# Turned activations of the second token chunk through memory in 512-byte pieces: attention mixer with a gated MLP on one core

## The chip, the cores and the metric

The kernel runs on one core of a Trainium2 chip. The metric is the device time of one execution in microseconds (us), the median of several runs of the same program. A profile is one further execution, taken by the hardware profiler. The engines are TensorE (PE; its weight loads are PEld), VectorE (DVE), ScalarE (ACT), GpSimd (POOL) and SyncE (SP), which here issues every DMA, one after the other, in the order of its instruction list.

## The reference

All tensors are float32; `x` is one sequence of 2048 tokens with 512 channels.

```python
xn = _layernorm(x)
s  = A(xn, wqkv, wo)          # 32 heads of 16, causal window of 256, softmax, projection wo
g  = silu(B(xn, w1, b1, w2, b2))
return x + s * g

def B(x, w1, b1, w2, b2):     # 512 -> 1792 -> 512, per token
    y = _layernorm(x)
    h = gelu(y @ w1 + b1)     # tanh form
    return h @ w2 + b2
```

## The kernel before

*Arithmetic.* Every matmul of float32 data is done as three passes of a split value: a tile is held as a high part in a short format and a low part, the difference (`split`, lines 69 to 72: a copy by the named engine, then a subtraction on DVE). `PASSES` gives high-high, high-low, low-high.

*Stages.* The first stage (lines 811 to 849) is the attention over all heads, with the first chunk's MLP weights prepared beside it. The second stage, from line 852, works in four chunks of 512 tokens each, c = 0 to 3; only the chunks 0 and 1 are computed by the loop of lines 1081 to 1179, the chunks 2 and 3 together by the code from line 1181 on. The change concerns what chunk 0's pass prepares for chunk 1, and chunk 1's gelu.

*One chunk of the loop.* For a step i over the 14 groups of 128 hidden units, `activate` (line 1091) applies gelu on ACT to a hidden tile h of 128 units by 512 tokens, then splits it into `gh` (ACT's cast) and `gl` (DVE's subtraction); `project` (line 928) multiplies the group of the step before with `w2` into four PSUM banks `acc`, 12 matmuls; `hidden` (line 1086) makes a later group's h with 12 matmuls. In chunk 0 most hidden groups were made in the first stage, so that its last steps are `project` alone. After the loop `end_chunk` (line 938) adds the bias to `acc`, applies silu (`gated`), and multiplies by the attention's projection `s`, 48 matmuls, whose inputs `ohl` were prepared by DVE in the steps i = 8 to 13.

*The turned y.* The matmuls of `hidden` need the normalised tokens of their chunk with channels on the partitions. For chunk 1 the tokens are loaded into four tiles `y` (128 tokens by 512 channels each, line 872) and normalised once more: statistics on DVE and the application on ACT in the steps i = 3 and 4 of chunk 0. `turn_y(1, range(4))` (line 1129) then transposes each tile in place by DVE, in blocks of 32 by 32, and writes it to `z_d` in memory, one DMA of 128 rows of 2 KB for each tile. A transposition in blocks leaves the blocks themselves where they were; `fetch_y` (line 894) puts them in their places with four DMAs for each of the four channel groups kt, each of 512 pieces of 128 bytes: sixteen DMAs (lines 1136 and 1137). They land in `mlp["yy"][1][kt]`. Line 1139 splits these tiles in the steps i = 12 (kt = 0), 13 (kt = 1) and 14 (kt = 2 and 3); the profile names the tiles `yh` and `xnT`, after the buffers they lie in.

*The sums and the outputs of the attention.* In the same steps chunk 0 needs the attention outputs divided by their sums. The reciprocals of the sums (`den`) are made by DVE in four parts, in the steps i = 4 and 5, written to memory (`rden_d`, line 1134), and for each group g of eight heads, `load_o` (line 901) loads the outputs (`or`, 256 KB) and the reciprocals of eight heads, each repeated for 16 rows (`w<-rden_d`, 256 KB, into free parts of a `w2` buffer). DVE multiplies the two (line 1146) and splits the product (`split_o`).

*Order on the queues.* In the loop all engines, SyncE among them, run their instructions in the order in which the program issues them. Around the change SyncE's list is: four `z_d<-y`, `rden_d<-den`, then `or`, `w` four times in turn, the sixteen `xnT<-z_d`, and, from behind the loop, the four y loads for chunk 2 and the four `xo` loads of chunk 0's end. DMAs report to eight semaphores in turn, and each one waits until the DMA eight places ahead of it has landed. A tile of pool `t2` (5 buffers) or `yp` (4 buffers: `y`, and `or` in chunk 0) waits until the tile that held its buffer has been used up. The buffer with the tag `wa` holds, one after another, a weight (`wva`), y of chunk 0, split hidden tiles (`g_first`, used up in the steps i = 1 and 2 of chunk 0) and from the end of chunk 0 on `gated`.

All instructions are recorded by one helper, so the profile gives line 43 for each; tiles tell them apart.

Of the kernel before, what the change touches and what calls it, by code (L numbers as in the profile page):

```python
# [9 lines left out]
F32 = mybir.dt.float32  # L10
F32R = mybir.dt.float32r
I32 = mybir.dt.int32
AF = mybir.ActivationFunctionType
# [4 lines left out]
S, D, H, DH, WIN, F = 2048, 512, 32, 16, 256, 1792  # L18
P = 128
NCH = S // 512  # L20
# [30 lines left out]
def mixer_kernel(ctx, tc, x, wqk, wv, wo, w1, b1, w2, b2, out):  # L51


    nc = SimpleNamespace(**{name: Ordered(tc, name) for name in ("tensor", "vector", "scalar", "gpsimd", "sync")})

    const = ctx.enter_context(tc.tile_pool(name="const", bufs=1))
    bigp = ctx.enter_context(tc.tile_pool(name="bigp", bufs=1))
    t2 = ctx.enter_context(tc.tile_pool(name="t2", bufs=5))
    small = ctx.enter_context(tc.tile_pool(name="small", bufs=3))
    dram = ctx.enter_context(tc.tile_pool(name="dram", bufs=1, space=bass.MemoryType.DRAM))  # L60
# [8 lines left out]
    def split(dst_hi, dst_lo, src, eng=None):  # L69

        (eng or nc.scalar.copy)(dst_hi, src)
        nc.vector.tensor_sub(dst_lo, src, dst_hi.bitcast(F32))
# [4 lines left out]
    def load(pool, tag, src, name, shape=(P, 512)):  # L77
        t = pool.tile(list(shape), F32, tag=tag, name=name)
        nc.sync.dma_start(t, src)
        return t  # L80
# [102 lines left out]
    oT_d = dram.tile([4, 8, 32, S], F32, name="oT_d")  # L183
# [2 lines left out]
    w_d = {"w1": dram.tile([P, NF * 512], F32, name="w1_d"), "w2": dram.tile([P, NF * 512], F32, name="w2_d"),  # L186
           "wo": dram.tile([P, 4 * 512], F32, name="wo_d")}
    g_d = dram.tile([NF, P, 512], F32, name="g_d")
    z_d = dram.tile([NCH - 1, 4, P, 512], F32, name="z_d")
    mT_d = dram.tile([NQ, NCH, 32, P], F32, name="mT_d")  # L190


# [45 lines left out]
    b1s = const.tile([P, NF], F32, name="b1s")  # L238
# [346 lines left out]
    mlp = {}  # L585
# [54 lines left out]
    def y_steps(a, b):  # L640
        run(mlp["ln"][a:b])

    def hidden_mm(ps, f, k):
        kt, (a, b) = k // 3, PASSES[k % 3]
        nc.tensor.matmul(ps, w1_part(a, f)[:, P * kt: P * (kt + 1)], mlp["yy"][b][kt],
                         start=(k == 0), stop=(k == 3 * KT - 1))
# [49 lines left out]
    n, raw = raws["qk"]  # L696
# [176 lines left out]
    for f in range(6, NF, 2):  # L873
        t = gp.tile([P, 2, 512], F32, tag="ohl", name=f"hr_{f}", bufs=4)
# [12 lines left out]
    def turn_y(c, tiles):  # L887

        for i in tiles:
            y = mlp["y"][i]  # L890
            nc.vector.transpose(y, y)
            nc.sync.dma_start(z_d[c - 1, i], y)

    def fetch_y(c, kt, dst):

        for k in range(4):
            at = z_d[c - 1, 0, 0, 128 * kt + 32 * k: 128 * kt + 32 * k + 32]
            nc.sync.dma_start(dst[32 * k: 32 * k + 32].rearrange("p (t j) -> p t j", j=32),
                              bass.AP(tensor=at.tensor, offset=at.offset, ap=[[512, 32], [32 * 512, 16], [1, 32]]))

    def load_o(c, g):

        cols = slice(512 * c, 512 * (c + 1))
        pool, tag = (t2, "t2") if c else (mlp["yp"], "y")
        raw = load(pool, tag, oT_d[g, :, 0:DH, cols], f"or_{c}_{g}")
        rec = mlp["w2", g // 2][:, 512 * (14 + g % 2): 512 * (15 + g % 2)].bitcast(F32)
        nc.sync.dma_start(rec, bass.AP(tensor=rden_d.tensor, offset=rden_d.offset + 8 * g * S + 512 * c,
                                       ap=[[S, 8], [0, DH], [1, 512]]))
        return raw, rec

    def split_o(c, g, raw):
        ohl = gp.tile([P, 2, 512], F32R, tag="ohl", name=f"ohl_{c}_{g}", bufs=4)
# [6 lines left out]
    def open_accs(c):  # L919
        return [ps_mx.tile([P, 2, 512], F32, tag="mx", name=f"acc_{c}_{i}") for i in range(2)]  # L920

    def split_g(c, f, g, cast):
        gh = gp.tile([P, 512], F32R, tag="gh", name=f"gh_{c}_{f}")
        gl = gp.tile([P, 512], F32R, tag="gl", name=f"gl_{c}_{f}")
        split(gh, gl, g, cast)
        return gh, gl
# [154 lines left out]
    for c in range(2):  # L1081
        accs = open_accs(c)
        gs, os_, hs, wanted = {}, [], {}, []
        made = ready if c == 0 else {}

        def hidden(f):
            hs[f] = (ps_yt if c and f % 2 else ps_st).tile([P, 512], F32, tag="b", name=f"h_{c}_{f}")
            for k in range(3 * KT):
                hidden_mm(hs[f], f, k)

        def activate(f):
            if f in made and f in soon:
                gs[f] = made[f]
                return
            src = made[f] if f in made else hs.pop(f)
            g = src if f in made and f < 2 else t2.tile([P, 512], F32, tag="t2", name=f"g_{c}_{f}")
            nc.scalar.activation(g, src, AF.Gelu_apprx_tanh, bias=b1s[:, f: f + 1])
            gs[f] = split_g(c, f, g, nc.scalar.copy)

        order = [2, 3, 0, 1, 4, 5, *range(6, NF)] if c == 0 else [*range(NF)]  # L1100
        ahead = 2 + c
        for f in range(ahead if c else 0):
            hidden(f)
        o_from, o_late = (0, 0) if c else (7, 1)
        nc.sync.on = True
        for i in range(NF + 1):
            if i < NF:
                activate(order[i])
            if c and i in (1, 2, 6, 7):
                y_steps(6, 10)  # L1110
            if c and i >= 10 and i < 14:
                second_y(i - 10)
            if c and i == 14:
                kept["w"] = bigp.tile([P, 768], F32R, tag="wb1", name="wsh")
                combine_w(0)
            if c == 0:
                for kind, f in late_w[LATE[i]: LATE[i + 1]]:
                    settle(kind, f, nc.scalar.copy, nc.vector)
            if i >= 1:
                project(accs, [(order[i - 1], gs.pop(order[i - 1]))], order[0], order[-1])  # L1120
            if i + ahead < NF and order[i + ahead] not in made and order[i + ahead] > 1:
                hidden(order[i + ahead])
            if c == 0:
                if i == 3:
                    mlp["ln"] = layernorm(mlp["y"], "C1", True)
                    y_steps(0, 5)
                if i == 4:
                    y_steps(5, 10)
                    turn_y(1, range(4))
                if i in (4, 5):  # L1130
                    for j in (2 * i - 8, 2 * i - 7):
                        nc.vector.reciprocal(den[:, P * j: P * (j + 1)], den[:, P * j: P * (j + 1)])
                if i == 5:
                    nc.sync.dma_start(rden_d.rearrange("g a (c t) -> (g a c) t", c=NCH), den)
                    wanted += [load_o(0, g) for g in range(4)]
                    for kt in range(KT):
                        fetch_y(1, kt, mlp["yy"][1][kt].bitcast(F32))
                for kt in {12: (0,), 13: (1,), 14: (2, 3)}.get(i, ()):
                    split(mlp["yy"][0][kt], mlp["yy"][1][kt], mlp["yy"][1][kt].bitcast(F32))
            else:  # L1140
                steps2(i)
            k = i - o_from
            if 0 <= k - 2 - o_late < 4:
                os_.append(split_o(c, k - 2 - o_late, wanted[k - 2 - o_late][0]))
            if 0 <= k - 1 - o_late < 4:
                nc.vector.tensor_mul(wanted[k - 1 - o_late][0], *wanted[k - 1 - o_late])
            if c and 0 <= k < 4:
                wanted.append(load_o(c, k))
            if c == 0 and i == NF:
                mlp["y"] = load_y(2)  # L1150
            if c:
                if i in (2, 3, 7, 8):
                    turn_y(2 + i // 5, (0, 1) if i in (2, 7) else (2, 3))
                if i == 3:
                    mlp["y"] = load_y(3)
                    kept[0] = gated[:, 2:4]
                    kept[1] = bigp.tile([P, 2, 512], F32, tag="wb1", name="y2_21")
                    for kt in range(KT):
                        fetch_y(2, kt, kept[kt // 2][:, kt % 2])
                if i in (8, 9):  # L1160
                    for kt in (2 * i - 16, 2 * i - 15):
                        put("21" if kt > 1 else "11", kt % 2, kept[kt // 2][:, kt % 2])
                if i == 8:
                    fetch_second()
                if i == 12:
                    fetch_pair(0)
            if c and i in (0, 1, 5, 6):
                y_steps(5, 6)
        nc.sync.on = False
        if c == 0:  # L1170
            gated = bigp.tile([P, 4, 512], F32, tag="wa", name="gated")

        def between(i):
            if c == 1 and i in (1, 2):
                split_w(0, 2 * i - 2)
                split_w(0, 2 * i - 1)
        end_chunk(c, accs, os_, between)
        if c == 0:
            steps2(-1)
# [99 lines left out]
    for i in range(NF):  # L1279
# [9 lines left out]
        if 5 <= i < 9:  # L1289
            raw, rec = wanted  # L1290
# [37 lines left out]
```

## Time and profile before

| | us |
|---|---|
| median of 3 runs | 746.75 (746.61 to 747.2) |
| the profiled execution, its own time | 746.98 |
| span of the profile | 745.2 |
| ACT busy | 440.1 |
| DVE busy | 516.5 |
| POOL busy | 297.5 |

The granted clock of TensorE is 1.00 over the whole span. The page of the profile gives the busy time of each engine, the span in 40 slices, and the chain of work that ended last, followed back from the last instruction to whatever released it. Views of the trace give the same for a stretch: the chain in order of time, an engine's instructions with the idle time before each one and its releaser, groups of instructions by shape with the mean of one in ns, and busy times with the share that the 16 DMA engines were busy and the GB/s that they moved. Times in the views are us from the start of the span. A row "SPq" is SyncE's work of issuing a DMA, not the transfer.

### The profile page before, as it was taken

Reading aid. Unit: us, or ns where it says so; the run is one execution under the profiler, and the core shown is the slowest. Engines: PE = TensorE matmul, PEld = TensorE weight load, DVE = VectorE, ACT = ScalarE, POOL = GpSimd, SP = SyncE. Lnnn points to the kernel's source line nnn. Section 1 sums busy time; section 2 is a strip of 40 time slices with the busy share of each in tenths; the row PEclk is TensorE's granted clock in tenths of the full one; section 3 lists DMA queues with packets and bytes.
Section 4 is the critical chain, followed back from the end, with each engine's and each line's share of the span. In section 5 each row is a group of like instructions: output and inputs, shape, how many; then the busy total and the mean of one; then the engine's idle time right before and its main releaser. Section 6 shows DMA issues by size and latency. Waiting matters only on the chain.

```text
span 745.2 us, 18812 instructions
## 1 busy us (share of the span) xinstructions
PE 728.8 (98%) x7360; PEld 585.6 (79%) x7360; DVE 516.5 (69%) x790; ACT 440.1 (59%) x744; POOL 297.5 (40%) x644
## 2 busy tenths in 40 slices
PE   8999999999999999999999999999999999999997
PEld 7886777777778887777776688788888888888886
DVE  6886777877766678887773567656658755676643
ACT  7757767867667676778877756443544734442001
POOL 7413757757666555767867700020102000001102
PEclk9999999999999999999999999999999999999999
DMA  8633355757555624646735385745453322253611
GB/s 289 192 71 77 86 137 149 210 151 194 142 133 153 154 71 149 163 129 165 201 103 161 92 286 201 198 143 194 110 108 113 96 88 74 69 181 117 214 55 56
DMA packets 84025, 105.71 MB, mean 142 GB/s; under 512 B 36640, under 2 KB 36896, under 8 KB 83936
## 3 DMA queue, kind: packets, MB, share of 16 engines
q1 hardware_dynamic: 83936, 104.50, 49.5%
q8 instruction: 58, 0.95, 0.5%
q14 instruction: 31, 0.25, 0.1%
HBM read 54.53 MB, written 32.77 MB: 117 GB/s over the span
## 4 chain that ended last, share of the span: by engine, by line
PE 86%; ACT 5%; DVE 3%; DMA 2%; issue 1%; POOL 1%; SPq 1%; DVEq 0%; ACTq 0%; POOLq 0%
PE fb L43 19%; PE acc L43 17%; PE zo L43 12%; PE stb L43 9%; PE p L43 9%; PE s L43 6%; PE h L43 6%; PE xy L43 5%; ACT pt L43 4%; PE pv L43 3%; POOL pt L43 1%; DVE xy L43 1%; SPq L43 1%; DMA w<-rden_d 1%; DMA xnT<-z_d 1%
## 5 line engine op out<-in xcount | busy, mean ns | idle before, releaser
L43 POOL TENSOR_SCALAR_AFFINE_SELECT pt<-pt 128x256 f32<-128x256 f32 x480 | 192.9, 425 | 133.7 <-ACT pt L43 131.7
L43 ACT ACTIVATE pt<-stb 128x768 f32<-128x768 f32 (+1 forms) x244 | 188.5, 773 | 62.4 <-PE stb L43 55.1
L43 DVE TENSOR_REDUCE mt<-xy 128x4 f32<-128x1024 f32 (+1 forms) x128 | 152.6, 1192 | 4.4
L43 DVE COPY_PREDICATED xy<-upper,zo 128x512 f32<-128x512 int32 x112 | 77.8, 695 | 70.6 <-PE xy L43 63.1
L43 POOL TENSOR_TENSOR xo<-xo,gated 128x512 f32<-128x512 f32 x15 | 19.9, 1330 | 236.9 <-DVE gated L43 195.5
L43 PE MATMUL fb<-xnT,wqb 64*128 64x512 f32 (+1 forms) x684 | 104.6, 397 | 0.2
L43 PE MATMUL zo<-pt,vt 128*17 128x128 f32 x2880 | 103.7, 275 | 0.3 <-POOL pt L43 0.3
L43 PE MATMUL stb<-qk 64*128 64x384 f32 (+1 forms) x488 | 97.1, 393 | 6.2 <-ACT pt L43 3.9
L43 PE MATMUL acc<-w,gh 128*128 128x512 f32 x320 | 98.6, 389 | 0.4 <-ACT gh L43 0.4
L43 PEld LDWEIGHTS stb<-qk 64*128 64x128 f32 x488 | 45.8, 183 | 51.5 <-ACT pt L43 46.3
L43 PEld LDWEIGHTS zo<-pt,vt 128*17 128x17 f32 x2880 | 67.5, 97 | 15.6 <-issue 6.3
L43 PEld LDWEIGHTS fb<-xnT,wqb 64*128 64x128 f32 (+1 forms) x684 | 64.7, 185 | 11.0 <-DVE pjr L43 1.4
L43 PEld LDWEIGHTS acc<-w,gh 128*128 128x128 f32 x320 | 60.0, 188 | 13.1 <-ACT gh L43 0.8
L43 PE MATMUL acc<-w,gl 128*128 128x512 f32 x160 | 62.3, 390 | 1.0 <-DVE gl L43 1.0
L43 PE MATMUL xy<-qk 64*128 64x256 f32 (+2 forms) x536 | 58.4, 291 | 0.2
L43 PEld LDWEIGHTS xy<-qk 64*128 64x128 f32 x536 | 46.6, 185 | 6.6 <-issue 3.1
L43 ACT COPY oraw<-zo 128x128 f32<-128x128 f32 x128 | 34.0, 266 | 29.4 <-PE zo L43 28.7
L43 PE MATMUL s<-wos,ohl 128*128 128x512 f32 (+1 forms) x204 | 44.3, 376 | 0.0
L43 ACT ACTIVATE gated<-acc 128x512 f32<-128x512 f32 x16 | 8.7, 596 | 59.3 <-DVE acc L43 59.3
L43 PEld LDWEIGHTS s<-wos,ohl 128*128 128x128 f32 x204 | 36.8, 188 | 7.1
L43 PEld LDWEIGHTS zo<-qk 64*128 64x128 f32 x448 | 38.5, 185 | 4.6 <-issue 1.4
L43 ACT COPY p<-p 128x512 f32<-128x512 f32 x21 | 12.3, 585 | 48.9 <-PE p L43 41.2
(191 smaller groups left out, 1233.8 us busy)
## 6 DMA issues: line engine op xcount, KB each, us to landing
qk<-sh SPq DMA_DIRECT2D x128, 128.0 KB
qk<-pjr SPq DMA_DIRECT2D x64, 128.0 KB
oT_d<-oraw SPq DMA_DIRECT2D x32, 256.0 KB
w_d<-in_w_dram SPq DMA_DIRECT2D x14, 512.0 KB
x<-in_x_dram SPq DMA_DIRECT2D x16, 256.0 KB
or<-oT_d SPq DMA_DIRECT2D x16, 256.0 KB
w<-rden_d SPq DMA_DIRECT2D x16, 256.0 KB
xo<-in_x_dram SPq DMA_DIRECT2D x16, 256.0 KB
```

What stands on the lines that cost most here:

```text
L43: r = issue(*args, **kwargs)
```

## The change

For chunk 1 the turned y takes another way.

- The four transpositions no longer work in place. They write into one new tile `whole` (tag `wa`), 16 blocks of 32 channels by 4 tiles by 32 tokens: block b of tile j goes to `whole[:, b, j]`, so that an output has runs of 32 elements with a step of 128.
- The writes are issued one step later in the program, at i = 5, still ahead of the write of `rden_d`: four DMAs, one for each strip of 32 partitions, 512 pieces of 512 bytes each, into `zt_d`, which holds channels as rows of 512 tokens.
- The sixteen fetches become four DMAs of 128 rows of 2 KB. Their place in the program is the same, behind the reciprocals and the loads of the attention outputs.
- The tokens stand in `zt_d` in a mixed order (strip, tile, token). Chunk 1's hidden tiles have the same order in their columns; gelu reads them straight on and writes them in the order of the tokens, in runs of 32.
- `z_d` shrinks to the two chunks that still use it. `load_o` is divided into two functions that it calls; its loads and their order stay the same.

On the instruction lists of TensorE and POOL nothing is added, removed or moved. On DVE four transpositions have another output, on ACT fourteen gelus. SyncE's list has twelve DMAs fewer; behind the four loads the y loads of chunk 2 and the `xo` loads, which follow the fetch, stand in a slightly different order among themselves (`y`, `y`, `xo`, `y`, `xo`, `xo`, `y`, `xo` instead of four `y`, four `xo`).

```diff
-    z_d = dram.tile([NCH - 1, 4, P, 512], F32, name="z_d")
+    z_d = dram.tile([2, 4, P, 512], F32, name="z_d")
+    zt_d = dram.tile([S // 4, 512], F32, name="zt_d")
...
-            nc.sync.dma_start(z_d[c - 1, i], y)
+            nc.sync.dma_start(z_d[c - 2, i], y)
...
-            at = z_d[c - 1, 0, 0, 128 * kt + 32 * k: 128 * kt + 32 * k + 32]
+            at = z_d[c - 2, 0, 0, 128 * kt + 32 * k: 128 * kt + 32 * k + 32]
...
-            nc.scalar.activation(g, src, AF.Gelu_apprx_tanh, bias=b1s[:, f: f + 1])
+            to = g
+            if c:
+                src = src.rearrange("p (a i t) -> p a i t", a=4, i=4)
+                to = g.rearrange("p (i a t) -> p a i t", a=4, i=4)
+            nc.scalar.activation(to, src, AF.Gelu_apprx_tanh, bias=b1s[:, f: f + 1])
...
                 if i == 4:
                     y_steps(5, 10)
-                    turn_y(1, range(4))
+                    whole = bigp.tile([P, 16, 4, 32], F32, tag="wa", name="y_1")
+                    for j, y in enumerate(mlp["y"]):
+                        nc.vector.transpose(whole[:, :, j], y.rearrange("p (b t) -> p b t", t=32))
...
                 if i == 5:
+                    for a in range(4):
+                        nc.sync.dma_start(zt_d[:, P * a: P * (a + 1)].rearrange("(b p) t -> p b t", p=32),
+                                          whole[32 * a: 32 * a + 32].rearrange("p b i t -> p b (i t)"))
                     nc.sync.dma_start(rden_d.rearrange("g a (c t) -> (g a c) t", c=NCH), den)
                     wanted += [load_o(0, g) for g in range(4)]
                     for kt in range(KT):
-                        fetch_y(1, kt, mlp["yy"][1][kt].bitcast(F32))
+                        nc.sync.dma_start(mlp["yy"][1][kt].bitcast(F32), zt_d[P * kt: P * (kt + 1)])
```

More of the change, by code (lines that the diff above doesn't have):

```diff
@@ L891, in turn_y, with load_raw, load_rec @@
             nc.vector.transpose(y, y)
[L892 removed]
+            nc.sync.dma_start(z_d[c - 2, i], y)
     def fetch_y(c, kt, dst):
         for k in range(4):
[L897 removed]
+            at = z_d[c - 2, 0, 0, 128 * kt + 32 * k: 128 * kt + 32 * k + 32]
             nc.sync.dma_start(dst[32 * k: 32 * k + 32].rearrange("p (t j) -> p t j", j=32),
                               bass.AP(tensor=at.tensor, offset=at.offset, ap=[[512, 32], [32 * 512, 16], [1, 32]]))
[L901 to L903 removed]
+    def load_raw(c, g):
         pool, tag = (t2, "t2") if c else (mlp["yp"], "y")
[L905 removed]
+        return load(pool, tag, oT_d[g, :, 0:DH, 512 * c: 512 * (c + 1)], f"or_{c}_{g}")
+    def load_rec(c, g):
         rec = mlp["w2", g // 2][:, 512 * (14 + g % 2): 512 * (15 + g % 2)].bitcast(F32)
@@ L908, in load_o @@
                                        ap=[[S, 8], [0, DH], [1, 512]]))
-        return raw, rec
+        return rec
+    def load_o(c, g):
+        return load_raw(c, g), load_rec(c, g)
     def split_o(c, g, raw):
```

## The prediction

> **What bounds the kernel now.** I read the page first, then TensorE's own timeline around the change, then the chain of waits there, and last the DMA share in short windows.
>
> ```profile
> PE 728.8 (98%) x7360; PEld 585.6 (79%) x7360; DVE 516.5 (69%) x790; ACT 440.1 (59%) x744; POOL 297.5 (40%) x644
> ...
> PE fb L43 19%; PE acc L43 17%; PE zo L43 12%; PE stb L43 9%; PE p L43 9%; PE s L43 6%; PE h L43 6%; PE xy L43 5%; ACT pt L43 4%; PE pv L43 3%; POOL pt L43 1%; DVE xy L43 1%; SPq L43 1%; DMA w<-rden_d 1%; DMA xnT<-z_d 1%
> ```
>
> TensorE (PE) is busy 728.8 of 745.2 us. The change leaves its list of matmuls as it is, so it can only take away idle time of TensorE, or add some. In the chain by line the fetch of the turned y (`xnT<-z_d`) has 1%, beside the reciprocal loads `w<-rden_d` that run ahead of it. This is where TensorE pays for it: first a row of the chain of waits (start, duration), then TensorE's timeline, with idle time and its releaser in brackets.
>
> ```profile
> 440.88 2.72 PE acc L43 x12
> ```
> ```profile
> 473.13 0.39 PE L43 MATMUL acc<-w,gl 128*128 128x512 f32 x1
> 473.88 0.73 PE L43 MATMUL acc<-w,gh 128*128 128x512 f32 x2 [0.36 <-ACT gh L43]
> 475.60 0.50 PE L43 MATMUL acc<-w,gl 128*128 128x512 f32 x1 [0.98 <-DVE gl L43]
> ...
> 478.00 11.04 PE L43 MATMUL s<-wos,ohl 128*128 128x512 f32 x48
> ```
>
> Twelve `acc` matmuls take 2.72 us, 0.227 each. The last group of chunk 0 should start at 473.13 + 0.23 = 473.36 and hand over to `s` at 473.36 + 2.72 = 476.08. It does so at 478.00: the stall costs **1.92 us**, and no more can be won at this place. Its cause, in the chain of waits and on ACT:
>
> ```profile
> 453.69 1.98 DMA rden_d<-den
> ...
> 455.68 6.14 DMA w<-rden_d
> ...
> 461.84 1.96 SPq L43
> ...
> 463.85 3.41 SPq L43
> ...
> 467.30 4.53 DMA xnT<-z_d
> ...
> 472.58 0.69 DVE xnT L43
> ...
> 474.94 0.62 DVE gl L43
> ```
> ```profile
> 471.93 0.62 ACT L43 CAST yh<-xnT 128x512 fp32r<-128x512 f32 x1 [3.37 <-DMA xnT<-z_d]
> ```
>
> The cast of the first turned tile (line 1139, i = 12) needs the first four of sixteen fetches. The fourth lands at 467.30 + 4.53 = 471.83, after ACT has stood idle for 3.37 us. Behind that cast wait, on ACT, the last gelu and `gh`; on DVE, behind the subtraction at 472.58, two `ohl` steps, an `or` product and `gl`, which TensorE gets at 475.60. Each microsecond by which the first tile lands earlier is worth one microsecond, up to 1.92; each by which it lands later costs one.
>
> **The change, part by part.** The writes first: SyncE's queue, then busy time and DMA in short windows (the last two columns are the DMA share and GB/s).
>
> ```profile
> 447.10 2.44 SPq L43 DMA_DIRECT2D z_d<-y  x4
> 453.69 0.32 SPq L43 DMA_DIRECT2D rden_d<-den  x1
> ...
> 461.19 15.22 SPq L43 DMA_DIRECT2D xnT<-z_d  x16
> 476.51 1.86 SPq L43 DMA_DIRECT2D y<-in_x_dram  x4
> ```
> ```profile
> 461.19 0.51 SPq L43 DMA_DIRECT2D xnT<-z_d  x1
> ```
> ```profile
> 446.36 2.83 DVE L43 STREAM_TRANSPOSE y<-y 128x512 f32<-128x512 f32 x4 [0.89 <-ACT y L43]
> ```
> ```profile
> 449.00:450.00 1.00, 1.00 (x6) 0.82 (x5) 1.00 (x3) 0.97 (x3) 0.00 (x0) 1.00 1.05 406
> ...
> 452.00:453.00 1.00, 1.00 (x6) 0.81 (x6) 1.00 (x2) 1.00 (x3) 0.00 (x0) 1.00 0.16 59
> 453.00:454.00 1.00, 1.00 (x6) 0.84 (x5) 1.00 (x2) 0.40 (x1) 0.00 (x0) 1.00 0.05 18
> 454.00:454.50 0.50, 0.50 (x4) 0.42 (x3) 0.50 (x2) 0.16 (x1) 0.00 (x0) 1.00 0.00 0
> 454.50:455.00 0.50, 0.50 (x3) 0.39 (x3) 0.31 (x2) 0.50 (x2) 0.00 (x0) 1.00 0.99 389
> ```
> ```profile
> 454.50:471.00 16.50, 16.50 (x74) 13.65 (x74) 10.21 (x17) 8.26 (x14) 0.00 (x0) 1.00 0.53 159
> 475.00:477.00 2.00, 1.40 (x6) 1.18 (x7) 1.97 (x4) 0.62 (x1) 0.00 (x0) 1.00 0.79 124
> 465.00:467.00 2.00, 2.00 (x10) 1.67 (x9) 1.60 (x4) 1.25 (x2) 0.00 (x0) 1.00 0.59 193
> 470.00:471.00 1.00, 1.00 (x6) 0.84 (x5) 0.00 (x0) 0.00 (x0) 0.00 (x0) 1.00 0.19 32
> ```
>
> *Four writes in 512-byte pieces.* Each old write left after its own transposition, from 447.10 on. Each new one takes a strip of all four tiles, so none leaves before the last transposition ends, 446.36 + 2.83 = 449.19. An issue of 512 pieces takes 0.51 us (the first old fetch has 512 pieces too); four end at about 451.3, well before the issue of `rden_d` at 453.69, which waits for DVE. From that issue to its bytes at 454.50 are 0.8 us, so the new bytes flow from 449.2 + 0.8 = 450.0. How long 1.05 MB take in 512-byte pieces no row shows. Bounds: 2 KB pieces move 406 GB/s at a share of 1.05, 387 at a full one: 2.7 us. The 128-byte pieces of the old fetch move 124 at 0.79, 157 at a full one: 6.7 us. Read as a fixed time plus a time per byte, with 2048/387 = 5.29 ns and 128/157 = 0.82 ns per piece, a 512-byte piece takes 0.82 + 384 x 4.47/1920 = 1.71 ns, and 2048 of them 3.5 us: done at 453.5. The DMA engines are nearly empty from 452 to 454.5 (shares 0.16, 0.05, 0.00), and that gap hides it. Cost taken: **0**. Without the gap, or at the price of 128 bytes, the writes end at 456.7, and `rden_d`, due at 454.50, moves by 2.2 us with all behind it.
>
> The row shows DMA reaching 406 GB/s when 128 partitions are read; no row shows a large transfer from 32. The Trainium skill ("SBUF — State Buffer", Door 1: The DMA port swizzle) says that 32 partitions reach only 8 of 16 ports, with 189 GB/s measured for 1 MiB; by it the writes would take an estimated 5.5 us, end at 455.5, and the sum would be 1.0 us worse.
>
> *Four whole loads for sixteen.* They stay behind `rden_d` and the eight `or` and `w` loads, whose times the edit doesn't touch. So the first of them is issued at about 461.2, as the first fetch was; then it has to get past what is queued ahead of it. From 465 to 467 the share is 0.59 at 193 GB/s, half of what 406 at 1.05 shows: the `or` and `w` loads (eight rows of heads outermost) fill about half of the engines. From 454.50 to 471.00 flow 16.5 x 159 = 2.62 MB, which is `rden_d` (0.26), the eight loads (2.10) and the first four fetches (0.26); at 470 to 471 only 32 GB/s are left. So those fetches, issued from 461.19 on, ended right after the eight loads, and SyncE's issues of 1.96 and 3.41 us (0.51 for the first) show a queue that is full. I take it that a whole load also finishes only behind `w` of the last group. Its bytes are as many as those of the four fetches, 0.26 MB, half of them on the loaded engines: 0.13 MB at 193 GB/s are 0.7 us, against 1.7 us in 128-byte pieces at half of 157 GB/s. The gain lies between 0 (the small pieces are hidden in the backlog) and 1.0; the 4.53 us of one fetch are mostly backlog, so I take the middle, **-0.5**.
>
> The rows of that stretch show half of the share and a late end. The Trainium skill ("DMA: Bandwidth & Descriptors", Queues, rings and completion order) says that on each engine descriptors are consumed in ring order; that speaks against this change, and by it the sum stays near this -0.5, while without it the stall of 1.92 would go.
>
> *What follows from it.* The tiles for kt = 1 to 3 land one load apart, 0.7 us each at 193 GB/s for a half, where each took four fetches; nothing of them is late next. What is left of the stall remains on ACT's first cast. The loads of the next y leave SyncE before 476.51, behind the whole loads, and can delay none of them.
>
> *Transpositions and gelus with stepped outputs.*
>
> ```profile
> L43 ACT ACTIVATE g<-h,b1s 128x512 f32<-128x512 f32 x16 | 10.9, 679 | 2.5 <-PE h L43 2.4
> ...
> L43 DVE COPY pjr<-fb 128x512 f32<-128x512 f32 x13 | 8.8, 680 | 0.0
> L43 ACT COPY pjr<-fb 128x512 f32<-128x512 f32 x15 | 8.8, 585 | 2.1 <-PE stb L43 1.0 <-PE fb L43 0.7
> ...
> L43 DVE STREAM_TRANSPOSE y<-y 128x512 f32<-128x512 f32 x12 | 8.1, 699 | 1.2 <-ACT y L43 1.2
> L43 DVE STREAM_TRANSPOSE mT<-mh 128x32 f32<-128x32 f32 x32 | 6.5, 203 | 0.8 <-POOL mh L43 0.7
> ...
> L43 DVE COPY vt<-fb 128x512 f32<-128x512 f32 x4 | 2.7, 680 | 0.0
> L43 ACT COPY vt<-fb 128x512 f32<-128x512 f32 x4 | 2.4, 588 | 0.7 <-PE stb L43 0.5
> ```
> ```profile
> 513.39 0.62 ACT L43 CAST gh<-g 128x512 fp32r<-128x512 f32 x1 [4.20 <-PE acc L43]
> ```
>
> The copies into `vt` write runs of 16 elements with gaps, those into `pjr` write straight on: 680 and 680 ns on DVE, 588 and 585 on ACT. By these nearest rows runs of 32 cost nothing: **0** for both edits. The other end for the transpositions: sixteen blocks at the 203 ns of one small one, 3.2 us for 0.7, four times: 10 us, all in front of DVE's reciprocals and so of `rden_d`. For the gelus: 679 ns doubled, which ACT's idle 4.20 us in front of a `gh` in chunk 1 hides; without that cover 14 x 0.68 = 9.5 us.
>
> **The sum.** The profiled execution took 746.98 us (span 745.2, and 1.8 around it); 746.98 - 0.5 = 746.5, and since it stands 0.23 above the median of 746.75, the median comes to **746.3 us**.
>
> **The rivals.** *The stall goes wholly.* If the first whole load lands as fast as `rden_d` did, in 1.98 us, it is there at 463.2, and TensorE runs through: 746.75 - 1.92 = 744.8. It needs engines that take the load past the backlog, or a backlog that ends 1.5 us sooner. For it: the load is one transfer where four were, and the chain ends in it. Against it: 64 KB needed 4.53 us. 12%.
>
> *The writes run over (the other side).* If 512-byte pieces from 32 partitions flow at the per-byte price of 128-byte ones, `rden_d` is pushed from 454.50 to 456.7, the eight loads and the first tile with it: +2.2 - 0.5 = +1.7, 748.5; with no gain at the fetch 749.0. It decides from the point where the writes take over 4.5 us (233 GB/s). For it: they start 2 us later than the old ones, right ahead of the sums. Against it: the gap. 30%, of which a sixth stays within 0.2%.
>
> *Stepped transpositions are slow*: up to 10 us, 757; the copies speak against it. 8%.
>
> *Forecast*: as summed, 745.6 to 747.9 with the bounds of fetch and writes, 50%.
>
> **How the numbers follow.** A measurement of this kernel can tell some 0.2%, 1.5 us, from no change. Faster: the first rival, 0.12. Within: forecast and a sixth of the second, 0.55. Slower: the rest of the second and the third, 0.33. The range runs from 744.9, next to the whole stall, to 749.2, just over the writes' rival; the slow transpositions and half of the first rival lie outside.
>
> **What would show it.** ACT's cast `yh<-xnT` with some 3 us of idle time before it confirms the backlog; near 469 and without idle time, the first rival. The issue of the first `w<-rden_d` after 456.5 would be the writes running over; `rden_d` issued after 453.7, slow transpositions; idle time of TensorE between 488 and 560, slow gelus. The prediction is wrong if the first whole load lands before 470.3 or after 473.4.

## The result and the profile after

| | before | after |
|---|---|---|
| median of 6 runs, us | 746.76 (746.35 to 747.2) | 749.66 (748.77 to 751.25) |
| the profiled execution, us | 746.98 | 749.99 |
| span of its profile, us | 745.2 | 748.3 |

The kernel after is slower: the ratio of its times to those of before is 1.0039, with a 95% interval of 1.0029 to 1.0049, 2.9 us. That lies just outside the predicted range (744.9 to 749.2), and the forecast of 746.3 had the kernel faster, not slower.

First the page of after, the busy times and the chain by line:

```profile
PE 729.9 (98%) x7360; PEld 585.9 (78%) x7360; DVE 516.7 (69%) x790; ACT 440.2 (59%) x744; POOL 298.6 (40%) x644
...
PE acc L43 19%; PE fb L43 18%; PE zo L43 11%; PE p L43 9%; PE stb L43 9%; PE s L43 6%; PE h L43 6%; PE xy L43 5%; ACT pt L43 4%; PE pv L43 3%; DMA xnT<-zt_d 2%; POOL pt L43 1%; DMA qk<-qk 1%; DVE xy L43 1%; DMA x<-in_x_dram 1%
```

The engines do the same work as before; TensorE is busy one microsecond longer in a span that is three longer. The fetch of the turned y has 2% of the chain where it had 1%. Then the chain of waits around the change (start, duration), TensorE's timeline and ScalarE's, with the idle time and its releaser in brackets:

```profile
463.52 11.24 DMA xnT<-zt_d
...
474.78 0.63 ACT yh L43
...
478.44 2.60 PE acc L43 x10
```
```profile
472.62 0.50 PE L43 MATMUL acc<-w,gl 128*128 128x512 f32 x1 [0.68 <-DVE gl L43]
...
476.72 0.73 PE L43 MATMUL acc<-w,gh 128*128 128x512 f32 x2 [1.52 <-ACT gh L43]
...
478.44 0.50 PE L43 MATMUL acc<-w,gl 128*128 128x512 f32 x1 [0.98 <-DVE gl L43]
...
480.88 1.30 PE L43 MATMUL s<-wos,ohl 128*128 128x512 f32 x5
```
```profile
474.78 0.62 ACT L43 CAST yh<-xnT 128x512 fp32r<-128x512 f32 x1 [5.96 <-DMA xnT<-zt_d]
```

The stall is at the same place and has grown. The first turned tile lands at 463.52 + 11.24 = 474.76, where it landed at 471.83, and ScalarE stands idle for 5.96 us in front of its cast instead of 3.37. `s` starts at 480.88 instead of 478.00. Of these 2.88 us, 0.26 were there already before the change could act: the transpositions start at 446.62 in this profile and at 446.36 in the one of before. So **the stall grew from 1.92 to 4.54 us, by 2.62**, nearly the whole 2.9. (TensorE now pauses three times. The idle times in brackets sum to 3.18; the rest of 4.54 lies around the restarts, where a single matmul takes 0.50 us.) All comparisons of starts below take such offsets off, with the start of the transpositions as the mark.

Where the delay arises is read on VectorE (transpositions and products of `or` with the reciprocals) and on SyncE's queue of after, then on one row of VectorE of before:

```profile
446.62 2.83 DVE L43 STREAM_TRANSPOSE y<-y 128x512 f32<-128x512 f32 x4 [0.89 <-ACT y L43]
...
463.05 0.69 DVE L43 TENSOR_TENSOR or<-or,w 128x512 f32<-128x512 f32 x1 [1.07 <-DMA w<-rden_d]
...
467.55 0.69 DVE L43 TENSOR_TENSOR or<-or,w 128x512 f32<-128x512 f32 x1 [2.15 <-DMA w<-rden_d]
...
471.27 0.69 DVE L43 TENSOR_TENSOR or<-or,w 128x512 f32<-128x512 f32 x1 [1.36 <-DMA w<-rden_d]
```
```profile
449.48 2.94 SPq L43 DMA_DIRECT2D zt_d<-y  x4
453.94 0.34 SPq L43 DMA_DIRECT2D rden_d<-den  x1
...
456.56 0.59 SPq L43 DMA_DIRECT2D w<-rden_d  x1
...
463.52 4.32 SPq L43 DMA_DIRECT2D xnT<-zt_d  x4
```
```profile
468.03 0.69 DVE L43 TENSOR_TENSOR or<-or,w 128x512 f32<-128x512 f32 x1 [0.40 <-DMA w<-rden_d]
```

The transpositions take 2.83 us as before, and `rden_d` is issued at 453.94, later by the offset alone. But the first `w`, which waits for `rden_d` to land, leaves at 456.56 instead of 455.68: 0.62 later net. The third product starts, on the landing of its `w`, at 471.27 instead of 468.03, 3.0 later net. So the sums are pushed by 0.6, and the eight loads behind them lose another 2 us and more. Last the windows of after (the last columns are granted clock, DMA share and GB/s):

```profile
452.00:453.00 1.00, 1.00 (x7) 0.81 (x6) 1.00 (x2) 1.00 (x3) 0.00 (x0) 1.00 0.78 173
453.00:454.00 1.00, 1.00 (x6) 0.84 (x5) 1.00 (x3) 0.65 (x2) 0.00 (x0) 1.00 1.03 290
454.00:454.50 0.50, 0.50 (x4) 0.42 (x3) 0.50 (x2) 0.00 (x0) 0.00 (x0) 1.00 0.96 263
...
454.50:471.00 16.50, 16.39 (x73) 13.24 (x72) 9.08 (x15) 8.42 (x14) 0.00 (x0) 1.00 0.67 182
464.00:465.00 1.00, 1.00 (x6) 0.81 (x5) 0.97 (x3) 0.00 (x1) 0.00 (x0) 1.00 1.27 205
465.00:467.00 2.00, 2.00 (x10) 1.68 (x9) 0.40 (x1) 1.25 (x2) 0.00 (x0) 1.00 0.66 246
```

The gap in DMA from 452 to 454.5 is filled by the writes, which still flow when `rden_d` wants to start. Right after the first whole load is issued, from 464 to 465, the share is 1.27 at only 205 GB/s. The share counts a packet's whole time in the window in which it starts, so the packets that start there take longer than others. From 454.5 to 471 the rate is 182 GB/s where it was 159, so more bytes move than before, but not those that VectorE waits for.

### The profile page after: what moved, and what is told of

It reads as the page before. It is cut to its first block, busy times and chain, and to the rows that moved or that the text cites. A ratio compares the mean times of both kernels' runs of the same rounds, so it can differ in the third digit from the quotient of the medians.

```text
span 748.3 us, 18777 instructions
## 1 busy us (share of the span) xinstructions
PE 729.9 (98%) x7360; PEld 585.9 (78%) x7360; DVE 516.7 (69%) x790; ACT 440.2 (59%) x744; POOL 298.6 (40%) x644
## 4 chain that ended last, share of the span: by engine, by line
PE 86%; ACT 5%; DMA 4%; DVE 2%; POOL 2%; issue 1%; SPq 0%; DVEq 0%; ACTq 0%; POOLq 0%
PE acc L43 19%; PE fb L43 18%; PE zo L43 11%; PE p L43 9%; PE stb L43 9%; PE s L43 6%; PE h L43 6%; PE xy L43 5%; ACT pt L43 4%; PE pv L43 3%; DMA xnT<-zt_d 2%; POOL pt L43 1%; DMA qk<-qk 1%; DVE xy L43 1%; DMA x<-in_x_dram 1%
```

## The experiments

Two theories stood against each other at first. **W**: the late writes in 512-byte pieces, from strips of 32 partitions, push `rden_d` and everything behind it. **L**: the whole loads flow beside the `or` and `w` loads and slow them. Each experiment below is the kernel before or after with one edit.

### One part of the change at a time

**loads_alone**: before, with whole loads (as blocks, so that chunk 1's blocks are not put in their places).

```diff
-                        fetch_y(1, kt, mlp["yy"][1][kt].bitcast(F32))
+                        nc.sync.dma_start(mlp["yy"][1][kt].bitcast(F32), z_d[0, kt])
```

> The kernel before with only the four whole loads of 2 KB rows, read from its old z_d (so the blocks of chunk 1's turned y are not put in their places; the old in-place transpositions and row writes stay). Theory W (the late 512-byte writes from strips of 32 partitions push rden_d and all behind it, the loads are harmless): 0.3 to 1.0 us faster than before, ratio 0.9987 to 0.9996, the yh cast near 471.5 us. Theory L (whole loads flowing beside the or and w loads slow those down, the writes matter little): 1.5 to 2.3 us slower, ratio 1.002 to 1.003, DVE waits of 1 to 2 us for w<-rden_d as after the change.

Measured: 748.77 us (747.64 to 752.15, 10 runs), ratio 1.0027 (1.0012 to 1.0041). ScalarE, VectorE, TensorE and windows of its profile:

```profile
472.57 0.62 ACT L43 CAST yh<-xnT 128x512 fp32r<-128x512 f32 x1 [4.27 <-DMA xnT<-z_d]
```
```profile
469.11 0.69 DVE L43 TENSOR_TENSOR or<-or,w 128x512 f32<-128x512 f32 x1 [1.62 <-DMA w<-rden_d]
```
```profile
474.52 0.73 PE L43 MATMUL acc<-w,gh 128*128 128x512 f32 x2 [1.26 <-ACT gh L43]
...
476.24 0.80 PE L43 MATMUL acc<-w,gl 128*128 128x512 f32 x1 [0.98 <-DVE gl L43]
```
```profile
476.00:478.00 2.00, 1.76 (x4) 1.49 (x5) 1.97 (x5) 1.31 (x2) 0.00 (x0) 0.55 0.79 280
478.00:480.00 2.00, 2.00 (x7) 1.55 (x7) 1.97 (x4) 0.00 (x0) 0.00 (x0) 0.60 0.47 137
```

The writes are those of before, in time, and still the third `w` comes 1.3 us later net (469.11 against 468.03, offset -0.26) and the first tile 0.9 us later. So the whole loads alone slow the loads ahead of them, as L says. One rival has no run of its own: with four issues in place of sixteen SyncE also sends the loads of the next y sooner, the first at 466.94 here and at 469.63 in after, where it was 476.51. In after they cannot be the start of the delay, since the wait for the second `w` (2.15 us) was over at 467.55. The windows show something that neither theory had: behind a stall that was not the longest of this study, TensorE's granted clock drops to 0.55 and 0.60 for some 4 us (11 matmuls in 4 us where 17 or 18 fit). That is taken up below.

**strips_2k**: before, with the four writes late and by strips, but in 2 KB pieces, and the sixteen old fetches.

```diff
-                    turn_y(1, range(4))
+                    whole = bigp.tile([P, 4, 512], F32, tag="wa", name="y_1")
+                    for j, y in enumerate(mlp["y"]):
+                        nc.vector.transpose(whole[:, j], y)
...
+                    for a in range(4):
+                        nc.sync.dma_start(z_d[0, :, 32 * a: 32 * a + 32].rearrange("i p t -> p i t"),
+                                          whole[32 * a: 32 * a + 32])
```

> The kernel before with transpositions into one tile and four late writes of strips of 32 partitions, in pieces of 2 KB; the sixteen old fetches stay. Theory W, if it is the strips and their lateness: 0.5 to 2.5 us slower, rden_d landing later than 455.7 us. Theory W, if it is the pieces of 512 bytes, and theory L: within 0.3 us of before.

**pieces_512**: before, with the four early writes from 128 partitions in 512-byte pieces into rows with gaps, and the sixteen fetches.

```diff
+    zp_d = dram.tile([4, P, 4, 160], F32, name="zp_d")
...
+                    for j, y in enumerate(mlp["y"]):
+                        nc.vector.transpose(y, y)
+                        nc.sync.dma_start(zp_d[j, :, :, 0:P], y.rearrange("p (k t) -> p k t", k=4))
```

> The kernel before with its four early writes of 128 partitions each cut into pieces of 512 bytes (rows with gaps in memory); the sixteen old fetches stay, from the rows with gaps. Theory W, if it is the pieces: 0.5 us or more slower. If it is the strips and their lateness, and theory L: within 0.3 us of before, since the DMA gap from 452 to 454.5 us takes up the longer writes.

Measured: strips_2k 747.33 us (746.36 to 750.12), ratio 1.0013 (1.0 to 1.0026); pieces_512 748.58 us (746.87 to 751.22), ratio 1.0024 (1.0011 to 1.0036). SyncE of strips_2k, and ScalarE of both, strips_2k first:

```profile
455.80 0.60 SPq L43 DMA_DIRECT2D w<-rden_d  x1
```
```profile
471.62 0.62 ACT L43 CAST yh<-xnT 128x512 fp32r<-128x512 f32 x1 [3.29 <-DMA xnT<-z_d]
```
```profile
471.85 0.62 ACT L43 CAST yh<-xnT 128x512 fp32r<-128x512 f32 x1 [3.16 <-DMA xnT<-zp_d]
```

The strips push the landing of `rden_d`, on which the first `w` waits, by 0.34 us net (455.80 against 455.68, offset -0.22), but in neither kernel does the first tile come later than before: in these profiled executions W does not lengthen the stall at all. The medians do rise, by 0.13%, with an interval that reaches down to no change, and by 0.24%. Of the ten executions of pieces_512, five have a mean clock of 0.997 or less and take 748.93 to 751.22, the others 746.87 to 748.22; of strips_2k it is three of ten. So a good part of the rise comes with a lower clock; what makes the clock lower there the profiles, both with a mean clock of 0.999, do not show. The rise of pieces_512 cannot be put down to the writes alone, since its sixteen fetches also read rows with gaps. No run has the new writes, late, by strips and in 512-byte pieces, together with the old fetches.

### The queue order, and the backlog

**first_ahead**: before, with the four fetches of kt = 0 ahead of the last group's `or` and `w`. **first_ahead_after**: after, with the first whole load there. The edit of the second (the first has `fetch_y(1, 0, ...)` in that place):

```diff
-                    wanted += [load_o(0, g) for g in range(4)]
-                    for kt in range(KT):
+                    for g in range(4):
+                        if g == 3:
+                            nc.sync.dma_start(mlp["yy"][1][0].bitcast(F32), zt_d[0: P])
+                        wanted.append(load_o(0, g))
+                    for kt in range(1, KT):
```

> The kernel before with the four fetches of the first tile (kt = 0) ahead of the or and w loads of the last group; nothing else changed. Both theories hold that these fetches wait behind whatever SyncE has issued ahead of them: the first tile should then land near 469.5 us, ACT's cast stand idle under 1.5 us, and the kernel be 1.2 to 1.9 us faster, ratio 0.9975 to 0.9984. If the order on the queue doesn't set when the first tile lands, nothing changes.

> The kernel after, with the first whole load issued ahead of the last group's or and w; the other three stay where they are. Theory L: the cast yh comes near 469 to 470, the stall of TensorE falls by 1.5 to 2 us, but the loads beside or and w still slow these, so the last ohl pieces are late: near 747, 2 us below after. If the last w sets the stall and not the first turned tile, nothing is won: 749 to 750.

Measured: first_ahead 747.29 us (746.61 to 747.71), ratio 1.0007 (0.9998 to 1.0016); first_ahead_after 746.48 us (745.49 to 747.7), ratio 0.9999 (0.9987 to 1.001). ScalarE and TensorE of first_ahead:

```profile
468.63 0.62 ACT L43 CAST yh<-xnT 128x512 fp32r<-128x512 f32 x1 [0.47 <-DMA xnT<-z_d]
```
```profile
474.00 0.50 PE L43 MATMUL acc<-w,gl 128*128 128x512 f32 x1 [0.43 <-DVE gl L43]
...
483.65 2.57 PE L43 MATMUL s<-wos,ohl 128*128 128x512 f32 x10 [1.65 <-DVE gated L43]
```

ScalarE and VectorE of first_ahead_after:

```profile
470.59 0.62 ACT L43 CAST yh<-xnT 128x512 fp32r<-128x512 f32 x1 [1.65 <-DMA xnT<-zt_d]
```
```profile
473.51 0.69 DVE L43 TENSOR_TENSOR or<-or,w 128x512 f32<-128x512 f32 x1 [0.50 <-DMA w<-rden_d]
```

Two places further up in the queue bring the first tile 2.9 us earlier in the kernel before: it does wait for its turn behind `or` and `w`. The expectation for the kernel before, 1.2 to 1.9 us faster, missed all the same: the stall ahead of `s` is down to 0.43, but `gated` is now late, and a new stall of 1.65 us stands inside `s`. (ScalarE waits 2.65 us for the last of the other fetches, until 478.99, before it turns to `gated`.) In the kernel after the edit wins back all that the change had cost (ratio 0.9999 for 1.0039); there the last `w` is now what VectorE waits for, ahead of the last `gl`.

**three_held**: after, with the whole loads of kt = 1 to 3 held back until step i = 12.

```diff
+                if i == 12:
+                    for kt in range(1, KT):
+                        nc.vector.memset(mlp["yy"][1][kt].bitcast(F32)[:, 0:1], 0.0)
```

(Their three DMAs follow there in the program; the first stays where it is.)

> The kernel after, with the whole loads for kt = 1 to 3 held back until step i = 12 (VectorE writes one column of their tiles there, which the load has to wait for); the first whole load stays where it is. Theory L (the whole loads run on the idle half of the engines beside or and w and slow them): with three quarters of that traffic gone the last w lands near 472 instead of 474 and the first turned tile too, the stall falls by 1 to 2 us: 747 to 748.5. Theory W: the three loads do not matter, the cast yh stays at 474.8: 749.5. If holding makes the other three late themselves, a new wait shows at s or at the first chunk-1 matmul.

Measured: 747.25 us (745.96 to 749.97, 11 runs), ratio 1.0013 (1.0004 to 1.0022). VectorE and ScalarE:

```profile
468.86 0.69 DVE L43 TENSOR_TENSOR or<-or,w 128x512 f32<-128x512 f32 x1 [0.29 <-DMA w<-rden_d]
```
```profile
472.01 0.62 ACT L43 CAST yh<-xnT 128x512 fp32r<-128x512 f32 x1 [3.64 <-DMA xnT<-zt_d]
```

Against after, the third product comes 2.0 us earlier net (468.86 against 471.27, offsets -0.18 and 0.26) and the first tile 2.3 us earlier, though nothing about either was moved, only three loads that stood behind them. (The next y loads move too, since SyncE works in order: the first leaves at 471.57 instead of 469.63, after the third `w` has landed.) That decides for L. By the ratios, 1.0013 for 1.0039, holding these three loads back is worth 1.9 of the 2.9 us; the other 1.0 is left over, for the writes and the first load, and was not split by a run.

**dmajor_before** and **dmajor_after**: both kernels, with the rows of `or` and `w` in another order. The 16 channels of a head become the outermost dimension of these loads instead of the eight heads; the rows of `wo` follow.

```diff
-        raw = load(pool, tag, oT_d[g, :, 0:DH, cols], f"or_{c}_{g}")
+        raw = load(pool, tag, oT_d[g, :, 0:DH, cols].rearrange("h d t -> d h t"), f"or_{c}_{g}")
...
-                                        ap=[[S, 8], [0, DH], [1, 512]]))
+                                        ap=[[0, DH], [S, 8], [1, 512]]))
...
-        "wo": np.asarray(A_wo).reshape(4, 2, 4, DH, D).transpose(0, 2, 1, 3, 4).reshape(4, P, D)
+        "wo": np.asarray(A_wo).reshape(4, 2, 4, DH, D).transpose(0, 3, 2, 1, 4).reshape(4, P, D)
```

> The kernel before, with the rows of the or and w loads in another order (the 16 channels of a head outermost, eight heads inside; the rows of wo follow), so that these loads fill all DMA engines and not half of them; all other DMAs as they are. Theory L (half-filled engines make the backlog in which the first turned tile waits, and leave the other half to whatever comes behind): each of the eight loads takes about 0.67 us instead of 1.34, the last w lands near 466 instead of 470.8, the first turned tile some 1 us behind it, the idle time of ScalarE before yh is gone, the stall of 1.92 us too: 744.8 to 745.3. If the time of the fetches is their own (sixteen issues, 128-byte pieces) and not the backlog, the cast stays at 471 to 472: 746.8.

> The kernel after, with the same order of the rows of or and w. Theory L: with all engines filled there is no idle half on which the whole loads could run beside the or and w loads and slow them; the last w lands near 466 to 467, the first turned tile near 467, the stall before s is gone and with it the drop of the clock: 744.8 to 745.5, 4 to 5 us below after. Theory W (the late writes alone set the time, by pushing rden_d and everything behind by about 0.6 us or more): the push stays, and no more than 1 to 2 us is won, 748 to 749.

Measured: dmajor_before 744.92 us (744.41 to 745.88, 11 runs), ratio 0.9977 (0.9968 to 0.9986); dmajor_after 744.93 us (744.61 to 745.3, 11 runs), ratio to before 0.998 (0.9971 to 0.9989). ScalarE, TensorE and the windows of dmajor_before, then the same of dmajor_after:

```profile
468.33 0.62 ACT L43 CAST yh<-xnT 128x512 fp32r<-128x512 f32 x1
```
```profile
475.95 6.28 PE L43 MATMUL s<-wos,ohl 128*128 128x512 f32 x27
```
```profile
454.50:471.00 16.50, 16.50 (x75) 13.66 (x74) 11.80 (x21) 9.75 (x17) 0.00 (x0) 1.00 0.78 183
```
```profile
469.72 0.62 ACT L43 CAST yh<-xnT 128x512 fp32r<-128x512 f32 x1 [1.19 <-DMA xnT<-zt_d]
```
```profile
476.05 6.28 PE L43 MATMUL s<-wos,ohl 128*128 128x512 f32 x27
```
```profile
454.50:471.00 16.50, 16.50 (x74) 13.68 (x73) 10.71 (x19) 9.47 (x17) 0.00 (x0) 1.00 0.90 249
```

In both the first tile lands early enough, the idle time in front of `s` is gone (no bracket), and the two kernels take the same time, by the ratios 4.4 us less than after and 1.5 to 1.7 less than before. The share from 454.5 to 471 rises to 0.78 and 0.90 from 0.53 and 0.67. The Trainium skill ("DMA: Bandwidth & Descriptors", Why a DMA increments its semaphore by 16 and not by 1) says that the number of DMA engines is the largest one up to 16 that divides the sizes of the slowest dimension on both sides: 8 with eight heads outermost, 16 with sixteen channels. The runs agree with it: in the semaphore updates that the traces record, each `or` and `w` load reports with eight updates as its bytes land (and one about 1 us after its issue) in before and after, and with sixteen in both dmajor kernels. So the edit does change the number of engines, and not only the order of the rows. In one thing the expectation missed: in dmajor_after the first whole load lands near 469.7 and not near 467, later than the four fetches of dmajor_before, whose cast starts at 468.33 without a wait. The change wins nothing of its own at this place; it is only that both are early enough.

### The clock behind a stall

The start of the cast, net of the offsets, gives the stall almost to a tenth. At 470.0 (471.93 - 1.92) there would be none; `s` would start at 476.08.

| kernel | cast yh starts, net | minus 470.0 | `s` starts, net, minus 476.08 |
|---|---|---|---|
| dmajor_before | 468.46 | none | 0.00 |
| three_held | 472.19 | 2.2 | 2.17 |
| after | 474.52 | 4.5 | 4.54 |
| loads_alone | 472.83 | 2.8 | 4.36 |

Of these four only loads_alone is off the line, by 1.5 us, and it is the one whose profile has the low clock. **stall_six** and **stall_nine** ask if the stall itself does it: dmajor_before, where all DMAs are early, with six or nine further copies of the cast.

```diff
+                if i == 12:
+                    for _ in range(6):
+                        nc.scalar.copy(mlp["yy"][0][0], mlp["yy"][1][0].bitcast(F32))
```

> The kernel of dmajor_before, with ScalarE's cast yh of the first turned tile done seven times instead of once (six further copies of 0.62 us each with the same source and target): a stall of TensorE made by ScalarE alone, with all DMAs early. In the kernel before the cast stood at 471.93 for a stall of 1.92; here the last of seven starts at about 468.3 + 3.7 = 472.0, so the stall is about 2.0 us. Theory C (a stall of TensorE alone can bring the granted clock down for some microseconds afterwards, whatever the DMAs do): 744.9 + 2.0 = 746.9, with single executions near 748.5 to 749 whose mean clock is 0.997. Rival D (the drop needs the DMA traffic of the slow kernels): 746.9 and no execution at 0.997.

> The same with nine further copies: 5.6 us, the last cast starts at about 473.9, the stall is about 3.9 us, as in the kernel after. Theory C: 744.9 + 3.9 = 748.8, and more than a quarter of the executions with a mean clock of 0.997 or less and 1.3 us or more above the others, 750 to 751. Rival D: 748.8 and all executions at 0.998 or more, within some 0.5 us of each other.

Measured: stall_six 747.89 us (747.28 to 749.36, 11 runs), stall_nine 751.88 us (750.67 to 752.59, 5 runs). The six and nine copies took 0.65 us each, so that the last cast starts some 0.4 us later than expected in both, for stalls of 2.4 and 4.3 us; with the 745.2 of dmajor_before in these runs (0.9977 x 746.96, their median of before) the sums without a drop are 747.6 and 749.5. Of the 11 executions of stall_six, seven have a mean clock of 0.999 or more and take 747.28 to 748.2; four have 0.997 and take 748.83 to 749.36. Of the five of stall_nine, one has 0.997 and takes 750.67, the others 0.995 and 751.16 to 752.59. TensorE and windows of stall_nine:

```profile
476.00 1.22 PE L43 MATMUL acc<-w,gh 128*128 128x512 f32 x2 [2.75 <-ACT gh L43]
```
```profile
474.00:476.00 2.00, 0.00 (x0) 0.00 (x0) 1.26 (x3) 1.94 (x5) 0.00 (x0) 0.84 0.78 260
476.00:478.00 2.00, 1.50 (x3) 0.78 (x4) 2.00 (x4) 1.98 (x4) 0.00 (x0) 0.50 0.24 62
478.00:480.00 2.00, 2.00 (x5) 1.54 (x6) 1.97 (x5) 0.81 (x1) 0.00 (x0) 0.50 0.20 73
480.00:482.00 2.00, 2.00 (x6) 1.59 (x5) 1.84 (x3) 0.09 (x1) 0.00 (x0) 0.50 0.76 240
```

The DMAs are those of dmajor_before, whose 11 executions all have a mean clock of 0.998 or more, and yet the clock falls: theory C holds. The drop begins inside the idle time (0.84 from 474 to 476) and lasts some 7 us. In stall_six the drop comes in four of eleven executions and puts these 1.4 to 1.9 us above the median of the others, 747.47; in stall_nine it comes in all five and lifts the median by 2.4 us over the sum.

## Why the prediction was wrong

- *What bounds the kernel* was right: the stall before `s`, set by the first turned tile. The tile landed at 474.76, past the 473.4 that was named as the bound. Its size follows the start of the cast to a tenth of a microsecond in the table above, but for the kernel with the low clock, and without it the time is 744.9, where the rival "the stall goes wholly" had 744.8.
- *The place in the queue* was right: the whole load waits behind `w` of the last group, and two places up brought the first tile 2.9 us forward in first_ahead. In after the semaphore updates show both halves of that load: eight come from 467.61 to 467.93, the other eight only from 471.35 to 474.75, behind `w`. The Trainium skill's ring order, cited with it ("DMA: Bandwidth & Descriptors", Queues, rings and completion order), agrees with that. But it does not protect the loads ahead, as the next point shows.
- *The whole loads* are where the prediction failed, in the words "whose times the edit doesn't touch", of the eight `or` and `w` loads. They are touched. With three of the four whole loads held back, `or` and `w` are 2 us earlier. The prediction saw that half of the engines were free and asked only what the new load would do there, not what it does to the loads on the other half; that term stood at nothing, without a reason. The step was worth about -0.5 in the sum; together with the loads it is about +2. The -0.5 for itself can be seen in one place: from the third `w` to the first tile go 474.75 - 471.25 = 3.5 us, where it was 471.83 - 468.0 = 3.8, so some 0.3.
- *The writes* were costed at 0 with the gap as cover, and the rival had them at +2.2. `rden_d` landed 0.62 us later: the fixed time plus a time per byte, 3.5 us for the four, was too short. By the windows from 452 to 454.5 the engines move 173 to 290 GB/s up to the end of the gap, which was to be empty, and the issues of the four writes end at 449.48 + 2.94 = 452.42, where 451.3 was expected. The Trainium skill's 189 GB/s for 32 partitions, cited there ("SBUF — State Buffer", Door 1: The DMA port swizzle), lies between these rows: from 452 to 453 only 173 flow, from 453 to 454 290. Its sum, 1.0 us worse, came nearer than mine. The sign that was named for the rival, a first `w` issued after 456.5, was met by a hair only (456.56, of which 0.26 are offset).
- *Transpositions and gelus* at 0 were right: 2.83 us for four in both profiles, `rden_d` issued 0.25 later, which is the offset, and the gelus' row for the whole kernel is word for word that of before:

```profile
L43 ACT ACTIVATE g<-h,b1s 128x512 f32<-128x512 f32 x16 | 10.9, 679 | 2.5 <-PE h L43 2.4
```

- *The clock* was in no part of the prediction: a stall was priced at its own length. Two of six executions of after show 0.997 and take 750.23 and 751.25, the four others 0.999 and 748.77 to 749.99. Without these two the median would be 749.1, so they move it by some 0.5 us; the profiled execution of after had none of it in the stall.
- *The range of the forecast itself* does not follow from its terms: a gain of 0 to 1.0 at the fetch and writes at 0 give 745.8 to 746.8, and not 745.6 to 747.9; where its upper end comes from is not said.
- *The sum by what was measured*: 0.6 for the pushed sums and some 2 for the slowed loads are the 2.6 us by which the stall grew; three_held puts 1.9 of the 2.9 us of the medians on three of the loads. The semaphore updates bear the split out. The mean of the eight with which the last `w` lands, net, is 469.28 in before, 469.92 in strips_2k (late writes only, in 2 KB pieces), 470.78 in loads_alone (whole loads only), 470.01 in three_held (late writes and one whole load) and 471.66 in after. So the late writes push these loads by some 0.6 and the whole loads behind them by some 1.5; together they give 2.4. (In strips_2k the push did not reach the first tile.)

What stays open is how the loads on the free half slow the other one. The bytes do not explain it, since 246 GB/s are far from the 406 that one window of before shows; the row of 464 to 465, with a share of 1.27 at 205 GB/s, shows slow packets, not their cause. It shows most in two of the eight updates of a load: for the third `w` of after six come from 466.60 to 468.03, the last two at 470.77 and 471.25, while in before all eight come from 465.84 to 468.01. Open too is what lowers the clock in half of the executions of pieces_512, whose profile shows no longer stall than before.

## What to carry to other kernels

A transfer that is sent behind others is not harmless to them: where loads fill only half of the DMA engines, ask what a better load behind them will do to their times, and first let those loads fill all engines, for example by a slowest dimension of 16 instead of 8. That one edit was worth more than the whole change, and made it pointless (744.9 with and without it). And price a stall of TensorE of some 2 us or more above its length, since the clock may drop behind it: here it did in four of eleven executions at 2.4 us and in five of five at 4.3 us.

## What the hardware showed unexpectedly

A stall in which TensorE still works for a moment can bring the clock down. In loads_alone the idle times are 1.26 and 0.98 us with two matmuls between them, and the clock falls to half; in after they are 1.52 and 0.98 us, and in the profiled execution the clock stays at 1.00. The same kernel has executions with and without the drop (four of eleven in stall_six, at a stall of 2.4 us).

The traces show a time grid behind this. The drop lasts 3.41 us in loads_alone (476.18 to 479.59) and 6.83, twice that, in stall_nine (475.36 to 482.19). In both it begins 471.04 us, which is 138 times 3.413, after the first entry in the trace's record of the clock (5.14 and 4.32). In the other ten profiles the full clock lasts 737.28 or 740.69 us from that entry, 216 or 217 times 3.413. Here are, for loads_alone, the window just ahead of the drop and the one in it, for stall_nine the one ahead of it, and the emptiest window around the stall on the same grid in after and in first_ahead. The first numbers are the window, its length and TensorE's busy time; the clock is the third from the end.

```profile
472.77:476.18 3.41, 1.23 (x5) 0.37 (x3) 2.92 (x6) 3.36 (x7) 0.00 (x0) 1.00 0.78 270
476.18:479.59 3.41, 3.35 (x8) 2.71 (x9) 3.38 (x7) 1.15 (x1) 0.00 (x0) 0.50 0.59 190
```
```profile
471.95:475.36 3.41, 1.30 (x6) 0.75 (x4) 0.66 (x2) 3.25 (x7) 0.00 (x0) 1.00 0.86 198
```
```profile
473.97:477.39 3.42, 1.90 (x8) 0.96 (x6) 1.93 (x4) 2.58 (x5) 0.00 (x0) 1.00 0.41 159
```
```profile
480.28:483.70 3.42, 1.77 (x9) 1.16 (x7) 3.35 (x7) 2.37 (x5) 0.01 (x1) 1.00 1.01 358
```

With TensorE busy for 1.2 or 1.3 us of such a window the clock is halved in the next one, with 1.8 or 1.9 us it is not. So it depends on where the idle time falls on the grid, and the grid lies differently in each execution: its first entry is between 4.32 and 6.44 us in the twelve profiles. By this reading it is luck that loads_alone lost its clock where after kept it. These are only four windows, and where between 1.3 and 1.8 us the limit lies they do not tell. The Trainium skill ("TensorE: Matmul & The Clock Gate", What's actually happening) describes a free-running window of about 3.4 us and a fall to half clock after an idle one. The length and the 0.50 agree with it. But the two windows ahead of a drop were not idle, only 36 and 38% busy, and no idle time in these stalls was longer than 2.75 us without a break; by these runs a stall that is kept under 3.4 us is not safe.
